# Attention units reordered and paced over half output steps, and a third pair's q through the crossbar

## The chip, the core and the metric

The kernel runs on one core of a Trainium2 chip. The metric is the device time of one launch in microseconds (us), taken as the median of several runs. TensorE (PE, with its weight loads shown as PEld), VectorE (DVE), ScalarE (ACT), GpSimd (POOL) and SyncE (SP, here a queue that issues DMAs) run side by side and wait for each other by semaphores.

## The reference

The inputs q, k and v have shape (4, 8, 768, 64): 4 batches, 8 heads, 768 rows, 64 columns. The rows form 8 blocks of 96. A small matrix `sort_net` (8 x 8 for each batch and head) becomes P by five rounds of row and column normalization. P mixes the blocks of k and of v, and each block of q attends to its mixed block. The result goes through a bilinear feed-forward network (FFN).

```python
k_sorted = einsum('bhij,bhjcd->bhicd', P, k_blocks)      # the same for v
attn = softmax(q_block @ k_sorted_block.T / sqrt(64))    # 96 x 96 in each block
x = (attn @ v_sorted_block)  ->  (4*768, 8*64)
out = ((x @ w_a) * (x @ w_b)) @ w_out                    # 512 -> 1536 -> 512
```

The matrix products run in bf16; sums are float32 in PSUM.

## The kernel before, in words

**The work.** Heads are taken in pairs. A pair has a number g = 4 * batch + pair, so batch 0 has g = 0 to 3 and batch 3 has g = 12 to 15. Batch 0 is computed in two halves of four blocks each (the `half_...` functions). Batches 1 to 3 take whole pairs, and each pair is cut into three units:

- `c_(g)`: `stage_mix` mixes k and v of the pair with P (12 + 12 matmuls into two PSUM tiles `mix`). ACT copies the k tile to `kT`; DVE and ACT copy one half each of the v tile to `vT`. For g > 4 SP then issues a DMA transpose (the crossbar) of `vT` into `vs`. For g = 4, 5 and 6 the unit begins with `turn_q`, which transposes q on PE by 12 matmuls into `q_ps` and copies it out on DVE. From g = 6 on POOL copies one element of `kT` into `gate`, which makes it wait, and then issues the loads of pair g + 2.
- `s_(g)`: `stage_scores` computes the scores in two halves of 8 matmuls, each into its own PSUM tile `sc`, and ACT takes the exponential of each. For g = 4 `turn_v` transposes v on PE.
- `o_(g)`: `stage_o` multiplies by v in two halves of 8 matmuls, each into its own PSUM tile `o_ps`. For each half DVE takes a reciprocal (`rec`) and multiplies (`xp`), which empties the tile. `to_xT` then issues a DMA transpose of `xp` into `xT` on SP.

For pairs whose q goes by the crossbar, `pair_q` reorders q on POOL (tile `qc`) and `stage_q` issues its DMA transpose on SP (tile `qTf`). Before, that holds for g = 7 to 15. `pair_q(7)` stands on POOL after the early loads, `stage_q(7)` in `s_(5)`, and for later pairs both stand in `o_(g-2)`.

**PSUM.** Pool `psA` has two slots of two banks. Every `mix`, `sc` and `o_ps` takes one, so each unit takes both, and a unit's first tile waits until the unit before has emptied its first tile, and likewise for the second. Pool `psF` has four slots of one bank for the FFN tiles `pf` and `po` and for `q_ps`.

**The FFN.** `ffn_ab(b, m, t)` is one step of 8 matmuls with 384 columns (4 for w_a, 4 for w_b); ACT copies the first product to `a_sb` and DVE multiplies it with the second into `hT`. `ffn_out(b, c)` is 12 matmuls with 512 columns into one `po`, which ACT (even c) or DVE (odd c) copies to `o_sb`, and SP stores it.

**Order.** PE, POOL and SP run in the written order. For the main part, `paced` goes through the steps of batch b's FFN and puts the 12 units of batch b + 1 among them. A step of `ab` counts 1 and a whole `ffn_out` counts 2. A unit is due when its share of the total is passed, and all units that are due after a step follow it at once. Before, the order of the units is c0 s0 c1 s1 o0 c2 s2 o1 c3 s3 o2 o3. ACT and DVE take their order in this part from a scheduler when the program is built.

**The begin of the FFN.** At the end of batch 0's first half five FFN accumulations are begun with three of their four matmuls: three in `psF` tiles and two in the halves of one `psA` tile named `two`. `ffn_ab` later adds the last matmul (line 332) to each.

Of the kernel before, what the change touches and what calls it, by code (L numbers as in the profile page):

```python
# [9 lines left out]
FP32 = mybir.dt.float32  # L10
# [6 lines left out]
def _ap(t: bass.AP, extra_offset, pattern):  # L17
    return bass.AP(tensor=t.tensor, offset=t.offset + extra_offset,
                   ap=[list(p) for p in pattern])
# [3 lines left out]
def kernel(  # L23
# [11 lines left out]
    nc = tc.nc  # L35
    P = 128
    B, H, S, D = q.shape
# [3 lines left out]
    DMODEL = H * D  # L41
# [4 lines left out]
    NCH = S // P  # L46
    HP = H // 2
    KA = DMODEL // P
    KO = DFF // P
# [17 lines left out]
    psA = ctx.enter_context(tc.tile_pool(name="psA", bufs=2, space=PSUM))  # L67
    psF = ctx.enter_context(tc.tile_pool(name="psF", bufs=4, space=PSUM))
# [19 lines left out]
    def load_pair(b, hp):  # L88
        tiles = []
        for name, t in (("k2", k), ("v2", v), ("q2", q)):  # L90
            base = (b * H + 2 * hp) * S * D
            if b == 0 and name == "q2":
                continue
            to = ld.tile([P, 2, W], BF16, tag=name, name=name)
            nc.gpsimd.dma_start(out=to, in_=_ap(t, base, [[W, P], [S * D, 2], [1, W]]))  # L95
            tiles.append(to)
        loaded[b * HP + hp] = tiles
# [3 lines left out]
    w_out_sb = const.tile([P, KO, DMODEL], BF16, name="w_out_sb")  # L101
# [8 lines left out]
    def load_out(c):  # L110
        nc.gpsimd.dma_start(
            out=w_out_sb[:, c * 4:(c + 1) * 4, :],
            in_=moe_w_out.rearrange("(kc p) n -> p kc n", p=P)[:, c * 4:(c + 1) * 4, :])
# [46 lines left out]
    def copy(eng, out, in_):  # L160
        if eng == "act":
            nc.scalar.copy(out=out, in_=in_)  # L162
        else:
            nc.vector.tensor_copy(out=out, in_=in_)  # L164
# [79 lines left out]
    def pair_q(g):  # L244
        qc = qtp.tile([P, NCH, 2, D], BF16, tag="qc", name="qc", bufs=4)
        nc.gpsimd.tensor_copy(out=qc.rearrange("p c e d -> p e c d"),  # L246
                              in_=loaded[g][2].rearrange("p e (c d) -> p e c d", c=NCH))
        st[g, "qc"] = qc

    def stage_q(g):  # L250
        qT = qtp.tile([P, NCH, P], BF16, tag="qTf", name="qTf", bufs=4)
        nc.sync.dma_start_transpose(out=qT, in_=st[g, "qc"].rearrange("p c e d -> p (c e d)"))
        st[g, "qT"] = qT

    def turn_q(g, eng="dve"):
        q2 = loaded[g][2] if g >= HP else q_first[:, 2 * g:2 * g + 2]
        q_ps = psF.tile([P, NCH, P], BF16, tag="F", name="q_ps")
        for c in range(NCH):
            for e in range(2):
                nc.tensor.matmul(q_ps[e * D:(e + 1) * D, c, :],  # L260
                                 lhsT=q2[:, e, c * D:(c + 1) * D],
                                 rhs=ident, is_transpose=True)
        qT = qtp.tile([P, NCH, P], BF16, tag="qT", name="qT")
        copy(eng, qT, q_ps)
        st[g, "qT"] = qT

    def turn_v(g):
        vT, vs = vTs[g % NBUF], vss[g % NBUF]
        vs_ps = psF.tile([P, NB, P], BF16, tag="F", name="vs_ps")
        for i in range(NB):  # L270
            nc.tensor.matmul(vs_ps[:, i], lhsT=vT[:, i], rhs=ident, is_transpose=True)
        nc.vector.tensor_copy(out=vs[0:BLK, :, V0:V0 + P], in_=vs_ps[0:BLK])
# [37 lines left out]
    def stage_o(g):  # L310
        xp = att.tile([BLK, NB, 2, D], BF16, tag="xp", name="xp")
        for hf in range(2):
            one_o(eTs[g % NBUF], hf, vss[g % NBUF], hf * NBH, xp, NB)
        st[g, "xp"] = xp
# [8 lines left out]
    hTs = {}  # L323
# [32 lines left out]
    def ffn_last(b, c):  # L356
        hT = hTs[b]
        rows = out[b * S:(b + 1) * S, :].rearrange("(p c) n -> c p n", c=NCH)
        for n0, n1, eng, queue in ((0, 384, "act", nc.sync), (384, DMODEL, "dve", nc.scalar)):
            po = psF.tile([P, 512], FP32, tag="F", name="po")  # L360
            for m in range(KO):
                nc.tensor.matmul(po[:, 0:n1 - n0], lhsT=hT[:, m, c * P:(c + 1) * P],  # L362
                                 rhs=w_out_sb[:, m, n0:n1], start=(m == 0), stop=(m == KO - 1))
            o_sb = ffp.tile([P, 512], FP32, tag="o_sb", name="o_sb", bufs=3)
            copy(eng, o_sb[:, 0:n1 - n0], po[:, 0:n1 - n0])
            queue.dma_start(out=rows[c][:, n0:n1], in_=o_sb[:, 0:n1 - n0])

    def ffn_out(b, c):
        if b == B - 1 and c == NCH - 1:
            ffn_last(b, c)  # L370
            return
        hT = hTs[b]
        po = psF.tile([P, DMODEL], FP32, tag="F", name="po")
        for m in range(KO):
            nc.tensor.matmul(po, lhsT=hT[:, m, c * P:(c + 1) * P], rhs=w_out_sb[:, m, :],  # L375
                             start=(m == 0), stop=(m == KO - 1))
        o_sb = ffp.tile([P, DMODEL], FP32, tag="o_sb", name="o_sb", bufs=3)
        copy("act" if c % 2 == 0 else "dve", o_sb, po)
        if b == 0:
            h, u = divmod(c, 3)  # L380
            for c2 in range(2):
                nc.sync.dma_start(
                    out=_ap(out, (h * PH * NCH + 2 * u + c2) * DMODEL,
                            [[NCH * DMODEL, PH], [1, DMODEL]]),
                    in_=o_sb[c2 * PH:(c2 + 1) * PH])
        else:
            rows = out[b * S:(b + 1) * S, :].rearrange("(p c) n -> c p n", c=NCH)
            nc.sync.dma_start(out=rows[c], in_=o_sb)


    with tc.manual_schedule(engines={ET.PE, ET.Pool, ET.SP}):
        with tc.manual_schedule(engines={ET.Activation, ET.DVE}):
# [7 lines left out]
            for it in range(5):  # L400
# [15 lines left out]
                if it > 0:  # L416
                    nc.tensor.matmul(heat[0:NB, 1, 0:NB], lhsT=rsum, rhs=rsum,
                                     start=True, stop=True)
# [59 lines left out]
            half_x(0, 2, "act")  # L478
            half_o(0, 3)
            begun = [psF.tile([P, 512], FP32, tag="F", name="pf") for _ in range(3)]  # L480
            two = psA.tile([P, 2, 512], FP32, tag="A", name="two")
            begun += [two[:, 0], two[:, 1]]
            for n, (m, w_sb) in enumerate(((0, w_a_sb), (0, w_b_sb), (1, w_a_sb),
                                           (1, w_b_sb), (2, w_a_sb))):
                if n == 3:
# [9 lines left out]
        load_pair(1, 3)  # L495
        for c in range(3):
            load_out(c)
        pair_q(2 * HP - 1)
        for g in range(2, 4):
            spread(nc.gpsimd, p_col, g * 8, 8)  # L500
# [22 lines left out]
        def units_full(b):  # L523
            g0, us = b * HP, []

            def c_(g):
                if g < 2 * HP - 1:
                    turn_q(g)
                stage_mix(g, "k", ("act",))
                stage_mix(g, "v", ("dve", "act"))  # L530
                if 2 * HP - 2 <= g < B * HP - 2:
                    nc.gpsimd.tensor_copy(out=gate, in_=kTs[g % NBUF][0:1, 0:1])  # L532
                    load_pair((g + 2) // HP, (g + 2) % HP)

            def s_(g):
                stage_scores(g)
                if g == HP:
                    turn_v(g)
                if g == HP + 1:
                    stage_q(2 * HP - 1)  # L540

            def o_(g):
                stage_o(g)
                to_xT(g)
                if 2 * HP <= g + 2 < B * HP:
                    pair_q(g + 2)
                    stage_q(g + 2)

            for n in range(HP + 1):
                if n < HP:  # L550
                    us.append(lambda g=g0 + n: c_(g))
                    us.append(lambda g=g0 + n: s_(g))
                if n > 0:
                    us.append(lambda g=g0 + n - 1: o_(g))
            return us

        def interleave(steps, units, spare, slow=0):
# [6 lines left out]
                    done += 1  # L564

        def paced(ab, po, units, spare):
            steps = [(1, f) for f in ab] + [(2, f) for f in po]
            total = sum(t for t, f in steps) - 2 * spare
            now = done = 0
            for t, step in steps:  # L570
                step()
                now += t
                while done < len(units) and done * total < now * len(units):
                    units[done]()
                    done += 1

        steps = [lambda: ffn_ab(0, 0, 0, begun[0:2]), lambda: ffn_ab(0, 1, 0, begun[2:4]),
                 lambda: ffn_ab(0, 2, 0, begun[4:5])]
# [3 lines left out]
        for b in range(B):  # L582
            ab = [lambda m=m, t=t, b=b: ffn_ab(b, m, t)
                  for m in range(KO) for t in range(2) if b > 0 or t == 1]
            po = [lambda c=c, b=b: ffn_out(b, c) for c in range(NCH)]
            paced(ab, po, units_full(b + 1) if b + 1 < B else [], 3 if b == 0 else 2)


# [28 lines left out]
```

## Time and profile before

| | |
|---|---|
| median of 3 runs | 247.38 us (247.31 to 247.84) |
| the profiled execution: its time, its span | 247.31 us, 245.5 us |
| PE busy | 236.9 us, 96% of the span |
| PEld, DVE, ACT, POOL busy | 137.5, 109.1, 104.4, 60.6 us |
| granted TensorE clock, mean | 1.000 |

The span runs from the first to the last instruction; 1.8 us of the execution's time lie outside it. A busy share is an average over the whole span. Which engine bounds a stage is read from the chain of waits, which follows the work that ended last back to its start, and from the waits of PE in that stage.

### The profile page before, as it was taken

To read this page: it belongs to the slowest core of one execution; us is meant where nothing else is said; L and a number is where in the kernel's file an instruction comes from. 1 tells how busy PE (TensorE), PEld (TensorE's weight loads), DVE (VectorE), ACT (ScalarE), POOL (GpSimd) and SP (SyncE) were. 2 spreads that over 40 slices of the span, in tenths; PEclk is the share of its full clock that TensorE was granted. 3 is DMA by queue.
4 is the path that set the end of the run, shared out by engine and by line. 5 is a ranking of instruction groups with operands and counts; after the bars stand their busy time and mean duration, and the time that the engine had idled before them with its cause. 6 is when DMAs were issued, how large, how long until landed. Compare 5 with 4: busy or idle time off the path is not lost.

```text
span 245.5 us, 5508 instructions
## 1 busy us (share of the span) xinstructions
PE 236.9 (96%) x2246; PEld 137.5 (56%) x2258; DVE 109.1 (44%) x259; ACT 104.4 (43%) x204; POOL 60.6 (25%) x87
## 2 busy tenths in 40 slices
PE   7888899999989999999999999999999999999995
PEld 2466566666645456666645466666645465665443
DVE  6674366656435243463616144454516144443210
ACT  3664764465651046545440055555540033333001
POOL 8876477700323021404041032210000000000000
PEclk9999999999999999999999999999999999999999
DMA  5999999946859968939394936934333310000122
GB/s 81 201 199 197 197 199 202 206 73 77 143 107 202 151 138 133 137 70 136 70 144 124 217 69 115 138 66 45 64 89 117 117 45 0 0 3 1 43 107 106
DMA packets 53129, 27.82 MB, mean 113 GB/s; under 512 B 29936, under 2 KB 50160, under 8 KB 53104
## 3 DMA queue, kind: packets, MB, share of 16 engines
q0 software_dynamic: 20944, 14.16, 40.7%
q1 hardware_dynamic: 32016, 13.25, 24.7%
q8 instruction: 17, 0.28, 0.4%
q10 hardware_dynamic: 144, 0.07, 0.1%
q14 instruction: 8, 0.07, 0.1%
HBM read 28.32 MB, written 6.29 MB: 141 GB/s over the span
## 4 chain that ended last, share of the span: by engine, by line
PE 94%; DVE 3%; issue 1%; ACT 1%
PE pf L332 51%; PE po L375 24%; PE mix L281 4%; PE o_ps L231 3%; PE heat L168 2%; PE sc L302 2%; PE mixh L180 2%; PE po L362 1%; PE vs_ps L208 1%; PE sc L195 1%; PE xt_ps L222 1%; PE q_ps L260 1%; PE two L332 1%; PE mixh L168 0%; ACT qT L162 0%
## 5 line engine op out<-in xcount | busy, mean ns | idle before, releaser
L353 DVE TENSOR_TENSOR hT<-a_sb,pf 128x384 bf16<-128x384 bf16 x95 | 52.6, 553 | 73.6 <-PE pf L332 48.5
L332 PE MATMUL pf<-xT,w_a_sb 128*128 128x384 bf16 x380 | 77.8, 326 | 0.0
L332 PE MATMUL pf<-xT,w_b_sb 128*128 128x384 bf16 x380 | 77.4, 326 | 0.0
L352 ACT CAST a_sb<-pf 128x384 bf16<-128x384 f32 x95 | 45.5, 479 | 62.1 <-PE pf L332 40.8
L375 PE MATMUL po<-w_out_sb,hT 128*128 128x512 bf16 x265 | 60.5, 379 | 0.7 <-issue 0.2
L332 PEld LDWEIGHTS <-w_b_sb 128*128 128x128 bf16 x384 | 37.5, 98 | 25.2 <-issue 0.6
L332 PEld LDWEIGHTS <-w_a_sb 128*128 128x128 bf16 x384 | 34.9, 98 | 22.2
L375 PEld LDWEIGHTS <-hT 128*128 128x128 bf16 x276 | 26.3, 97 | 30.3
L162 ACT COPY o_sb<-po 128x512 f32<-128x512 f32 (+1 forms) x13 | 7.5, 578 | 50.0 <-PE po L375 48.6
L164 DVE COPY o_sb<-po 128x512 f32<-128x512 f32 (+1 forms) x12 | 7.9, 658 | 44.3 <-PE po L375 38.7
L307 ACT ACTIVATE eT<-sc 96x768 bf16<-96x768 f32 x24 | 18.1, 803 | 3.2 <-PE sc L302 3.2
L532 POOL COPY gate<-kT 1x1 bf16<-1x1 bf16 x8 | 1.4, 179 | 68.8 <-ACT kT L162 68.8
L237 DVE TENSOR_TENSOR xp<-o_ps,rec 96x512 bf16<-96x512 f32 x24 | 15.7, 683 | 0.2
L162 ACT CAST kT<-mix 128x384 bf16<-128x384 f32 x24 | 10.3, 482 | 8.1 <-PE mix L281 8.1
L95 POOL DMA_DIRECT2D k<-in_k_dram x16 | 11.6, 726 | 5.1 <-PE pf L332 2.3
L95 POOL DMA_DIRECT2D v<-in_v_dram x16 | 11.5, 721 | 2.5 <-PE pf L332 0.7
L231 PEld LDWEIGHTS <-eT 96*128 96x128 bf16 x256 | 10.4, 97 | 2.7 <-issue 0.2
L246 POOL COPY qc<-q 128x768 bf16<-128x768 bf16 x9 | 7.6, 840 | 17.3 <-DMA q<-in_q_dram 17.3
L231 PE MATMUL o_ps<-vs,eT 96*128 96x65 bf16 x256 | 11.2, 193 | 0.0
L95 POOL DMA_DIRECT2D q<-in_q_dram x12 | 8.7, 721 | 1.6 <-DMA w_a_sb<-in_moe_w_a_dram 0.7
L168 PE MATMUL heat<-warm 128*128 128x512 bf16 x20 | 7.6, 527 | 1.4 <-DVE warm L77 1.3
L164 DVE CAST vT<-mix 128x384 bf16<-128x384 f32 x12 | 6.7, 558 | 3.9 <-PE mix L281 3.8
(80 smaller groups left out, 154.0 us busy)
## 6 DMA issues: line engine op xcount, KB each, us to landing
out_dram<-o_sb SPq DMA_DIRECT2D x17, 256.0 KB, 2.0
k<-in_k_dram POOLq DMA_DIRECT2D x16, 192.0 KB, 5.1
v<-in_v_dram POOLq DMA_DIRECT2D x16, 192.0 KB, 6.3
q<-in_q_dram POOLq DMA_DIRECT2D x12, 192.0 KB, 6.4
w_a_sb<-in_moe_w_a_dram POOLq DMA_DIRECT2D x6, 256.0 KB, 10.1
w_b_sb<-in_moe_w_b_dram POOLq DMA_DIRECT2D x6, 256.0 KB, 10.4
w_out_sb<-in_moe_w_out_dram POOLq DMA_DIRECT2D x3, 512.0 KB, 10.0
out_dram<-o_sb SPq DMA_DIRECT2D x12, 128.0 KB, 2.4
```

What stands on the lines that cost most here:

```text
L95: nc.gpsimd.dma_start(out=to, in_=_ap(t, base, [[W, P], [S * D, 2], [1, W]]))
L162: nc.scalar.copy(out=out, in_=in_)
L164: nc.vector.tensor_copy(out=out, in_=in_)
L168: nc.tensor.matmul(ps[:, 0:cols], lhsT=warm[:, 0:P], rhs=warm[:, 0:cols], start=True, stop=True)
L231: nc.tensor.matmul(o_ps[:, e, i * (D + 1):(i + 1) * (D + 1)], lhsT=eT[:, hf, e, i * BLK:i * BLK + P], rhs=vs[0:BLK, i0 + i, V0 - 1 + e * ( ...
L237: nc.vector.tensor_tensor(out=_ap(xp, i0 * 2 * D, [[nxp * 2 * D, BLK], [D, 2], [2 * D, NBH], [1, D]]), in0=_ap(o_ps, 1, [[1024, BLK], [511 ...
L281: nc.tensor.matmul(mix[e * D:(e + 1) * D, c // 3, c % 3 * P:(c % 3 + 1) * P], lhsT=src2[:, e, c * D:(c + 1) * D], rhs=s_all[:, 2 * g + e], ...
L307: nc.scalar.activation(out=eT[:, hf, :, 0:HB], in_=sc[0:BLK, :, 0:HB], func=AF.Exp, scale=float(scale))
L332: nc.tensor.matmul(pf[:, 0:HW], lhsT=w_sb[:, kc, m * P:(m + 1) * P], rhs=x_cols(b, kc, t), start=(kc == 0), stop=(kc == KA - 1))
L352: nc.scalar.copy(out=a_sb, in_=pf[:, 0:HW])
L353: nc.vector.tensor_mul(out=hT[:, m, t * HW:(t + 1) * HW], in0=a_sb, in1=ab[1][:, 0:HW])
L375: nc.tensor.matmul(po, lhsT=hT[:, m, c * P:(c + 1) * P], rhs=w_out_sb[:, m, :], start=(m == 0), stop=(m == KO - 1))
```

## The change

1. `ffn_out` becomes two steps of 6 matmuls each on the same `po`, and the store follows the second. `paced` counts every step 1, so a unit can fall between two halves.
2. The order of the units becomes c0 s0 c1 s1 c2 o0 s2 c3 o1 s3 o2 o3: the third and the fourth mix each come one unit sooner.
3. q of g = 6 no longer goes through `turn_q`: `pair_q(6)` comes before `pair_q(7)` on POOL and `stage_q(6)` into `s_(4)`.
4. For g >= 8 `pair_q` and `stage_q` move from `o_(g-2)` to `s_(g-1)`.
5. The two begun accumulations that shared one `psA` tile `two` take a tile each, both named `two`.

```diff
     def ffn_out(b, c):
         if b == B - 1 and c == NCH - 1:
-            ffn_last(b, c)
-            return
-        hT = hTs[b]
-        po = psF.tile([P, DMODEL], FP32, tag="F", name="po")
-        for m in range(KO):
-            nc.tensor.matmul(po, lhsT=hT[:, m, c * P:(c + 1) * P], rhs=w_out_sb[:, m, :],
-                             start=(m == 0), stop=(m == KO - 1))
+            return [lambda: ffn_last(b, c)]
+        held = {}
+
+        def part(n):
+            if n == 0:
+                held["po"] = psF.tile([P, DMODEL], FP32, tag="F", name="po")
+            for m in range(n * KO // 2, (n + 1) * KO // 2):
+                nc.tensor.matmul(held["po"], lhsT=hTs[b][:, m, c * P:(c + 1) * P],
+                                 rhs=w_out_sb[:, m, :], start=(m == 0), stop=(m == KO - 1))
+            if n == 1:
+                store(b, c, held["po"])
+
+        return [lambda: part(0), lambda: part(1)]
+
+    def store(b, c, po):
         o_sb = ffp.tile([P, DMODEL], FP32, tag="o_sb", name="o_sb", bufs=3)
...
-            two = psA.tile([P, 2, 512], FP32, tag="A", name="two")
-            begun += [two[:, 0], two[:, 1]]
+            begun += [psA.tile([P, 2, 512], FP32, tag="A", name="two")[:, 0] for _ in range(2)]
...
+        pair_q(2 * HP - 2)
         pair_q(2 * HP - 1)
...
             def c_(g):
-                if g < 2 * HP - 1:
+                if g < 2 * HP - 2:
                     turn_q(g)
...
                 if g == HP:
                     turn_v(g)
-                if g == HP + 1:
-                    stage_q(2 * HP - 1)
+                if g in (HP, HP + 1):
+                    stage_q(g + 2)
+                if 2 * HP <= g + 1 < B * HP:
+                    pair_q(g + 1)
+                    stage_q(g + 1)
 
             def o_(g):
                 stage_o(g)
                 to_xT(g)
-                if 2 * HP <= g + 2 < B * HP:
-                    pair_q(g + 2)
-                    stage_q(g + 2)
-
-            for n in range(HP + 1):
-                if n < HP:
-                    us.append(lambda g=g0 + n: c_(g))
-                    us.append(lambda g=g0 + n: s_(g))
-                if n > 0:
-                    us.append(lambda g=g0 + n - 1: o_(g))
+
+            for u, n in ((c_, 0), (s_, 0), (c_, 1), (s_, 1), (c_, 2), (o_, 0), (s_, 2), (c_, 3),
+                         (o_, 1), (s_, 3), (o_, 2), (o_, 3)):
+                us.append(lambda u=u, g=g0 + n: u(g))
             return us
...
         def paced(ab, po, units, spare):
-            steps = [(1, f) for f in ab] + [(2, f) for f in po]
-            total = sum(t for t, f in steps) - 2 * spare
-            now = done = 0
-            for t, step in steps:
+            steps = ab + po
+            total = len(steps) - 2 * spare
+            done = 0
+            for now, step in enumerate(steps, 1):
                 step()
-                now += t
                 while done < len(units) and done * total < now * len(units):
...
-            po = [lambda c=c, b=b: ffn_out(b, c) for c in range(NCH)]
+            po = [f for c in range(NCH) for f in ffn_out(b, c)]
```

## The prediction

> **What bounds the kernel now.** I read the page's head and its chain of waits first, to learn which engine sets the end; then PE's own waits in the main part, to learn where that engine stands still; then the chain piece by piece around those places.
>
> ```profile
> span 245.5 us, 5508 instructions
> PE 236.9 (96%) x2246; PEld 137.5 (56%) x2258; DVE 109.1 (44%) x259; ACT 104.4 (43%) x204; POOL 60.6 (25%) x87
> ...
> PE 94%; DVE 3%; issue 1%; ACT 1%
> ```
>
> PE is busy for 96% of the span and holds 94% of the chain. The rest of the chain is mostly the first 12 us, which the change does not touch. So time can only come from PE work taken away or from PE waits taken away. PE's waits from 28 us to the end:
>
> ```profile
> PE sc L302 <- ACT kT L162: 0.7, 1, 0.7
> PE sc L302 <- ACT vT L162: 0.2, 1, 0.2
> PE po L375 <- issue: 0.2, 1, 0.2
> ```
>
> All three belong to one place, 70 to 73 us. In the table of windows PE is busy 54.34 of 54.50 us in batch 1's FFN (86.8 to 141.3) and 54.44 of 54.60 in batch 2's: nothing is to be had there. Before 28 us one wait matters here, 0.6 us of `two` (line 332) for DVE's `hT`. The chain in order of time (start, duration, what):
>
> ```profile
> 26.29 0.52 PE mixh L180 x24
> 26.81 0.55 DVE hT L353
> 27.35 0.04 issue
> 27.39 0.32 PE two L332
> 27.72 0.65 PE pf L332 x4
> ...
> 60.37 0.46 PE q_ps L260 x12
> 60.83 0.67 PE mix L281 x24
> ...
> 70.44 0.81 PE mix L281 x24
> 71.25 0.02 issue
> 71.28 0.57 DVE vT L164
> 71.84 0.02 issue
> 71.87 0.49 ACT vT L162
> 72.36 0.04 issue
> 72.40 0.35 PE sc L302 x8
> 72.75 0.16 issue
> 72.90 2.54 PE po L375 x11
> ...
> 88.09 0.79 PE mix L281 x24
> ```
>
> At 26.8 PE stands until DVE has read the other half of the same tile. At 60.4 the transposes of q take 0.46 us of PE. At 70.4 c7 is followed at once by s7: a whole `ffn_out` counts 2, so two units came due together, and s7 finds both `psA` slots still being emptied. At 88.1 stands the price of a mix that needs no transposes.
>
> **The change part by part.**
>
> *q of g = 6 by the crossbar.* The q_ps and mix pieces of c6 took 0.46 + 0.67 = 1.13 us; a mix alone takes 0.79. PE gains **0.34 us**. The 0.55 us copy of `q_ps` leaves DVE, off the path. What is added: a copy on POOL (0.84 us by line 246) and a transpose on SP (1.24 us of SP, landing 2.8 to 4.4 us after issue). On POOL it stands where `qc` of g = 7 already waited 3.37 us for its load, until 44.71; if that cover were gone, 0.84 us would move the last two `s_all` spreads (45.50 to 49.46), first used at 88. Cost nothing. On SP it precedes the first `vs` transpose, issued at 55.16; with q copied by about 46 it has landed by 51, and s6 comes near 64. Cost nothing.
>
> The Trainium skill, "TensorE: Matmul & The Clock Gate", Part 4 (PE-mode transpose), gives about 275 ns for a 128x128 bf16 transpose inside a kernel, and by that the 12 would be an estimated 3.3 us and the change worth some 3 us more. The trace shows 12 of them (64-column weights, 128 columns out) in 0.46 us of chain, 38 ns each, since they overlap; the single row's 223 ns is latency, and I go by the chain.
>
> *Units over half steps, and the mix one unit sooner.* For batch 0 there are 12 + 12 steps, total 24 - 6 = 18, so the units fall after steps 1, 2, 4, 5, 7, 8, 10, 11, 13, 14, 16, 17, with one or two steps (1.30 us each: 8 matmuls of `pf`, or half of the 2.59 us of a `po`) between neighbours. Before, units 9 and 10 fell together. They took 70.44 to 72.75 = 2.31 us; c7 and s7 apart cost 0.79 + 0.45 = 1.24 (pieces at 88.09 and 64.20). That frees 1.07; but c7 is now followed by FFN steps, and a step after a mix takes 1.41 instead of 1.30 (pieces at 64.65 and 66.55; the one after scores shows the same). PE gains **0.96 us**.
>
> *`two` as two tiles.* The last matmul into the second half then need not wait for DVE's reading of the first. From the end of the mixes (26.81) to the next `pf` (27.72) is 0.91 us; one matmul after a mix takes 0.27 (the piece at 25.86). PE gains **0.64 us**. Next late could be the scores at 28.37, moved to 27.73: they need the slot of the first `two`, free when DVE ends at 27.36, so they do not wait. The second tile's slot is that of the last first-half `o_ps`; its reader `xph` also feeds the transposes at 23.44, which PE passes first, so no wait is added.
>
> Sum of the gains: 0.34 + 0.96 + 0.64 = 1.94 us.
>
> *New waits.* In batch 1 four pairs of neighbours now stand one step apart that did not: c6-o4, s6-c7, o5-s7, o6-o7. Each needs both `psA` slots of its predecessor.
> - c6-o4: after c7's start (70.44) ACT ended its part of `vT` at 72.35, 1.9 us later; o4's second half starts 0.79 + 1.41 + 0.25 = 2.45 after c6. No wait.
> - s6-c7: exponentials of s6 ended at 66.02, 1.82 after its start at 64.20; c7's second mix starts 0.45 + 1.41 + 0.4 = 2.26 after. No wait.
> - o5-s7: o7's last multiplication ended at 79.89 + 0.69 = 80.58, 2.05 after its start (78.53). s7's second half would start at 0.50 + 1.30 + 0.23 = 2.03, and a release takes 0.05 more (72.35 to 72.40): a wait of 0.07.
> - o6-o7: store 1's copy on DVE (0.69 us) still stands ahead of o6's reciprocals. In the trace o6 had just that: start 75.44, last multiplication ended at 77.59, 2.15 later. o7's second half would start at 0.50 + 1.30 + 0.25 = 2.05: a wait of 0.15.
>
> A wait also costs the restart: the 8 scores after one took 0.35 instead of 0.23, and 0.16 of issue followed. I take 0.1 for each, so **0.4 us** in all. From below it is 0 (both waits are of the size of my rounding); below nothing I exclude, since no PE work leaves by it. From above, DVE can have one more FFN multiplication (0.55) ahead in each: 0.4 + 1.1 = 1.5. I take 0.4, as the rows above are the same instructions in the same order.
>
> *q one unit sooner for g >= 8.* On POOL `qc` waits for its load, and behind it stand the `gate` and the loads of the next pair. For g = 8 the order is gate of c7, its three loads, `qc`, as it was (74.23, no wait); the q load of pair 8 is issued some 2 us earlier than before, c6 being earlier, and lands in 5 to 6.5 us. For g = 10 to 12 `qc` came after the next pair's loads without a wait (99.85, 112.21, 124.56) and has the same place. The 4.2 and 4.86 us that POOL waited at 79.26 and 130.28 become work of the next batch's first unit, hidden behind its loads. On SP `qTf` for g = 9 is issued some 5 us after c8's start (kT 1.1, gate and three load issues 2.7, copy 0.86) and lands 3 us later; s9 starts eight steps and three units, some 12 us, after c8. Nothing waits. If one did, `vs` and `xT` transposes and stores stand behind it on SP.
>
> *Batches 2 and 3.* 36 steps, total 32: units after steps 1, 3, 6, 9, 11, 14, 17, 19, 22, 25, 27, 30, never closer than two steps (2.6 us), against 2.15 us for the slowest emptying. The counts of mixes, scores and outputs among the steps are the same. Cost nothing. `xT`'s last transpose is issued near 78 in batch 1, before it was 82.39, and the FFN step that first reads it comes near 85.3, before it was 86.80: more room.
>
> Net: 1.94 - 0.4 = 1.5 us. The profiled execution took 247.31 (span 245.5 and 1.81 around it), so 245.8; the median of the runs is 0.07 above it, within the rounding: **245.8 us**.
>
> **The rivals.**
>
> *No new wait at all.* For it: the two waits rest on differences of 0.02 and 0.10 us. Then all of 1.94 stays: 245.4. Chance 0.17.
>
> *Half of it is given back.* The order of DVE puts FFN multiplications ahead in o5 and o6, or `two`'s wait is followed by another in the half stage, whose tiles also turn over in `psF`. Waits of 1.0 to 1.45: 246.4 to 246.9. Chance 0.10.
>
> *Only the transposes' share stays*, because the stall at 71 us moves to the new neighbours and the one at 27 us to the next tile: 247.38 - 0.34 = 247.0, no measurable change. Chance 0.08.
>
> *Slower: the two `psA` slots become the bound in batch 1.* Place: the four one-step pairs, 58 to 77 us. Price: at distance zero one pair cost 1.07 us, so 4.3 at most, against 1.94 gained: 249.7. It decides against the change when each pair waits over 0.61 us, that is when each emptying ends 0.6 us later than its second tile is wanted. For it: DVE serves FFN multiplications (0.55), vT, and outputs in one line, and PE follows at once. Against: two of the four have 0.45 us of room by the rows above. Chance 0.07.
>
> **How the numbers follow.** Forecast 0.58, no new wait 0.17, half given back 0.10, unchanged 0.08, slower 0.07. A change of 0.2%, 0.5 us, is about what a measurement of this kernel can tell from none. Faster than 246.9 are the first three: 0.85; within: 0.08; slower: 0.07. The range goes from 245.2 (no new wait, 0.11 saved at `two` where a restarted matmul is read as an ordinary one, and 0.11 after c7 not paid) to 246.9 (new waits at their upper bound of 1.5).
>
> **What would show it.** In the profile after: no `q_ps` pieces between 55 and 65 us; the mix near 65 followed by `pf`, not by scores; no PE wait for ACT's `kT`; no wait of `two` for `hT`; PE waits for DVE `xp` of 0.05 to 0.3 at s7 and o7, near 71 and 76; the first `pf` of the next batch's FFN near 85.3 instead of 86.80; and the chain from there as long as before. It is wrong if PE waits for a `qTf` or `vs` transpose, or if PE's waits after 28 us add up to more than 1 us.

## The result and the profile after

| | before | changed |
|---|---|---|
| median of 6 runs | 247.19 us (246.59 to 247.84) | 245.80 us (245.78 to 246.84) |
| the profiled execution: time, span | 247.31 us, 245.5 us | 246.84 us, 245.1 us |

The ratio of changed to before is 0.9951, 95% interval 0.9929 to 0.9974: faster by 0.3 to 0.7%, or 0.6 to 1.8 us. The forecast was 245.8 us, a gain of 1.5.

The head of the page and PE's own waits from 28 us on, after:

```profile
span 245.1 us, 5487 instructions
PE 236.8 (97%) x2234; PEld 137.1 (56%) x2246; DVE 109.4 (45%) x258; ACT 104.5 (43%) x204; POOL 61.4 (25%) x88
```

```profile
PE o_ps L231 <- DVE xp L237: 0.2, 1, 0.2
```

PE is still the bound. The three waits at 70 to 73 us are gone from this list; one new wait of 0.2 us stands in it, and it is o7's for the slot that o6's `xp` empties. The chain in order of time shows the rest (start, duration, what):

```profile
27.30 0.27 PE two L332
27.57 0.65 PE pf L332 x4
...
46.60 0.46 PE q_ps L260 x12
...
58.42 0.79 PE mix L281 x24
...
65.56 0.79 PE mix L281 x24
66.35 1.41 PE pf L332 x8
...
70.84 0.29 PE sc L302 x8
71.14 0.02 issue
71.16 0.34 PE sc L302 x8
...
74.23 0.69 DVE o_sb L164
...
75.11 1.26 DVE xp L237 x2
...
76.41 0.42 PE o_ps L231 x8
...
85.89 1.30 PE pf L332 x8
```

`two` (27.30) starts where the mixes end, with no DVE piece between, c6 (58.42) and c7 (65.56) cost 0.79 each, and c7 is followed by an FFN step. At s7 the two halves of the scores are split by a short wait. At o7 the chain leaves PE for DVE: the copy of store 1, the reciprocals and the multiplications of o6 stand in a line, and o7's second half starts when they end.

Since every run shifts the first 25 us a little, I compare stretches of the chain that start and end at the same work in both kernels. The rows of before that bound the batch 1 stretch, with o7 between them:

```profile
46.76 0.46 PE q_ps L260 x12
...
75.94 2.59 PE po L375 x12
78.53 0.50 PE o_ps L231 x16
...
86.80 1.30 PE pf L332 x8
```

| stretch | before | after | difference |
|---|---|---|---|
| end of the mixes to the next `pf`, near 27 us | 26.81 to 27.72 = 0.91 | 27.30 to 27.57 = 0.27 | -0.64 |
| c4's start to the first FFN step of the next batch (batch 1) | 46.76 to 86.80 = 40.04 | 46.60 to 85.89 = 39.29 | -0.75 |
| the same FFN's start to the next one's (batch 2) | 86.80 to 141.32 = 54.52 | 85.89 to 140.42 = 54.53 | 0 |
| and once more (batch 3) | 141.32 to 195.85 = 54.53 | 140.42 to 194.94 = 54.52 | 0 |

In the profiled executions PE gained 0.64 + 0.75 = 1.39 us in these stretches. The two profiled executions differ by only 0.47 us because the one of the changed kernel lost 0.5 us ahead of 25 us and 0.5 us after its last copy, in code that the change does not touch; the other five runs of the changed kernel took 245.78 to 245.82 us.

### The profile page after: what moved, and what is told of

It is laid out like the page before. It is cut to its first block, busy times and chain, and to the rows that moved or that the text cites. A ratio compares the mean times of both kernels' runs of the same rounds, so it can differ in the third digit from the quotient of the medians.

```text
span 245.1 us, 5487 instructions
## 1 busy us (share of the span) xinstructions
PE 236.8 (97%) x2234; PEld 137.1 (56%) x2246; DVE 109.4 (45%) x258; ACT 104.5 (43%) x204; POOL 61.4 (25%) x88
## 4 chain that ended last, share of the span: by engine, by line
PE 92%; DVE 4%; issue 1%; ACT 1%; DMA 1%
PE pf L332 51%; PE po L377 24%; PE mix L281 4%; PE o_ps L231 3%; PE sc L302 2%; PE mixh L180 2%; PE po L362 1%; PE vs_ps L208 1%; PE sc L195 1%; PE xt_ps L222 1%; DMA p_nat<-in_sort_net_dram 1%; PE heat L168 1%; PE two L332 1%; PE q_ps L260 1%; DVE xp L237 1%
## 5 line engine op out<-in xcount | busy, mean ns | idle before, releaser
L377 PE MATMUL po<-w_out_sb,hT 128*128 128x512 bf16 x265 | 61.3, 379 | 0.6
L95 POOL DMA_DIRECT2D v<-in_v_dram x16 | 11.5, 722 | 3.5 <-DMA w_b_sb<-in_moe_w_b_dram 1.8
L235 DVE RECIPROCAL rec<-o_ps 96x8 f32<-96x8 f32 x32 | 5.6, 189 | 13.8 <-PE o_ps L231 13.8
L246 POOL COPY qc<-q 128x768 bf16<-128x768 bf16 x10 | 8.4, 843 | 7.5 <-DMA q<-in_q_dram 7.5
```

Source lines behind the costliest of these rows:

```text
L377: nc.tensor.matmul(held["po"], lhsT=hTs[b][:, m, c * P:(c + 1) * P], rhs=w_out_sb[:, m, :], start=(m == 0), stop=(m == KO - 1))
```

## The experiments

The prediction summed three parts of the change as if each were worth its own PE time. The rival reading is that they depend on each other. All ratios below are to the kernel before, on the same chip, with their 95% intervals; "the batch 1 stretch" is the second row of the table.

### Each part alone

**`two_only`**: the kernel before with only this edit:

```diff
-            two = psA.tile([P, 2, 512], FP32, tag="A", name="two")
-            begun += [two[:, 0], two[:, 1]]
+            begun += [psA.tile([P, 2, 512], FP32, tag="A", name="two")[:, 0] for _ in range(2)]
```

> The kernel before, with only the two begun accumulations in a psA tile each. Three-gains theory (each part of the change takes its own PE time): 0.64 us faster than before; in the chain the last matmul into the second two takes 0.27 us after the mixes near 27 us, with no wait for hT; the pieces at 60 and 70 us stay as before (q_ps 0.46 + mix 0.67; c7 and s7 2.31). Moved-stall theory: the wait goes to the scores or the vs transposes behind it, PE's waits before 30 us stay at 0.6, time as before.

Measured: 246.52 us, ratio 0.9959 (0.9942 to 0.9975): a gain of 0.6 to 1.4 us. After the mixes `two` takes 0.27 us, as expected, and no wait follows it. But in the profiled execution the batch 1 stretch is longer than the 40.04 us of before: it runs from 45.56 to 85.93 and takes 40.37, 0.33 us more. PE's waits and the chain name the place:

```profile
PE o_ps L231 <- DMA vs<-vT: 0.2, 1, 0.2
```

```profile
71.19 6.18 DMA vs<-vT
...
77.51 0.65 PE o_ps L231 x16
```

o7 now waits for the transpose of g = 7's v, issued at 71.19 and in the chain for 6.18 us. In the kernel before, SP issued it here:

```profile
72.40 1.29 SPq L292 DMA_TRANSPOSE vs<-vT  x1
```

It landed 5.8 us later, at 78.2, and PE came to o7 at 78.53, 6.1 us after the issue: 0.3 us of room were left, and no wait showed. `two` stands ahead of the issue, so it moves the issue and o7 alike, and the 6.1 us between them are the same in both kernels. What differs is the landing, 6.2 us instead of 5.8. That the edit brings this about is not shown. The gain of the runs has room for the forecast 0.64 and none for 0.64 - 0.33 = 0.31.

**`q_only`**: the kernel before with only q of g = 6 by the crossbar:

```diff
+        pair_q(2 * HP - 2)
         pair_q(2 * HP - 1)
...
-                if g < 2 * HP - 1:
+                if g < 2 * HP - 2:
                     turn_q(g)
...
-                if g == HP + 1:
-                    stage_q(2 * HP - 1)
+                if g in (HP, HP + 1):
+                    stage_q(g + 2)
```

> The kernel before, with only q of g = 6 by POOL and the crossbar. Three-gains theory: 0.34 us faster; c6 takes 0.79 in place of 1.13, the wait at 70 us and the one of two stay. Late-q theory: s6 near 64 waits for qTf, or POOL's added copy holds back a later step; time as before or above. If the 12 transposes cost what a lone one costs (0.22 us by their rows), 2.6 us faster.

Measured: 247.32 us, ratio 1.0003 (0.9991 to 1.0016): nothing gained. The batch 1 stretch is 46.24 to 86.36 = 40.12. Neither theory foresaw why. The chain:

```profile
59.85 0.97 PE mix L281 x24
...
77.86 0.08 issue
77.94 0.65 PE o_ps L231 x16
```

c6 takes 0.97 instead of 0.79: in the old order o4 stands one step ahead of it, and without the 0.46 us of transposes between them its second tile comes before o4's slot is free. The rest goes at o7, where 0.50 becomes 0.08 + 0.65. The profile lists no wait there, but the `vs` transpose, issued at 71.72, took 6.1 us to land, and PE came to o7 just as long after the issue: again a landing 0.3 us longer than before, where before had 0.3 us of room. In the changed kernel c6 costs 0.79: there scores, two steps back, stand ahead of it and not outputs one step back.

**`halves_only`**: the old order of units, only `ffn_out` in two steps and every step counted 1 (part 1 of the change, as in its diff).

> The kernel before in the old order of units, with only the output steps halved and counted 1 each. Three-gains theory: c7 and s7 come apart, 0.96 us less there; o6 and o7 now stand one step apart with store 1's copy on DVE between, which costs 0.32 as in the changed kernel; net 0.6 us faster, and o5 and s7 are not neighbours, so no wait at s7. Order theory (the new order is what takes the stall away): under 0.2 us faster, since a wait for the psA slots stays near 70 us.

Measured: 247.13 us, ratio 0.9984 (0.9969 to 0.9999). c7 and s7 do come apart (c7 costs 0.79 at 68.87), but the batch 1 stretch is 46.48 to 86.34 = 39.86, a gain of 0.18 where some 0.6 was expected:

```profile
70.80 5.69 DMA vs<-vT
...
76.62 0.65 PE o_ps L231 x16
```

The wait for `vs` at o7 is 0.6 us by PE's waits, larger than the one for `xp` that I had expected. Here the cause is in the edit: the stall that it takes away stood between the issue of the transpose and o7. PE now comes to o7 5.2 us after the issue instead of 6.1, and the landing took 5.7.

The same two times in six profiles (room: from the issue of `vs` of g = 7 until PE has done the work ahead of o7; landing: from the issue to the arrival):

| kernel | issue | room | landing | wait for `vs` |
|---|---|---|---|---|
| before | 72.40 | 6.1 | 5.8 | none |
| `two_only` | 71.19 | 6.1 | 6.2 | 0.2 |
| `q_only` | 71.72 | 6.1 | 6.1 | 0.1 by the chain |
| `halves_only` | 70.80 | 5.2 | 5.7 | 0.6 |
| `old_order` (below) | 70.48 | 5.2 | 5.9 | 0.8 |
| changed | 67.49 | 8.5 | 7.0 | none |

The three parts alone change the batch 1 stretch and `two` together by -0.31, +0.08 and -0.18 us. Their sum is -0.41; the change as a whole gives -1.39. But the profile of `two_only` stands apart: these stretches give it 0.31 and the medians of the runs 0.81, while for every other kernel here except `q_late` the two agree within 0.2 us (`halves_only` 0.18 and 0.20). With `two` at its 0.64 the sum is -0.74. What the runs show to depend on other parts is the rest: q and the half steps, priced at 0.34 and 0.96 ahead of the new waits, give 0.10 alone.

### The order of the units

**`old_order`**: the changed kernel with only the order undone:

```diff
-            for u, n in ((c_, 0), (s_, 0), (c_, 1), (s_, 1), (c_, 2), (o_, 0), (s_, 2), (c_, 3),
-                         (o_, 1), (s_, 3), (o_, 2), (o_, 3)):
+            for u, n in ((c_, 0), (s_, 0), (c_, 1), (s_, 1), (o_, 0), (c_, 2), (s_, 2), (o_, 1),
+                         (c_, 3), (s_, 3), (o_, 2), (o_, 3)):
```

> The changed kernel with the units in the order of the kernel before (c0 s0 c1 s1 o0 c2 s2 o1 c3 s3 o2 o3), all other parts kept. Transpose theory (the earlier parts are worth something only because the new order issues the vs transpose of g = 7 sooner): from c4's start c7 begins at 22.2 us and vs is issued 1.9 later; it lands 5.7 after that, o7 cannot start before 30.0, so the FFN after it starts 39.7 us after c4's start against 39.3 in the changed kernel; PE waits some 1 us at o7 for vs. 0.4 us slower than the changed kernel, 1.0 faster than before. Independent-parts theory (the prediction, which priced the order at nothing but its new waits): o7 waits 0.3 for xp, s7 not at all; 0.2 faster than the changed kernel.

Measured: 246.61 us, ratio 0.9982 (0.9972 to 0.9993). The batch 1 stretch is 46.33 to 86.24 = 39.91, 0.62 more than in the changed kernel (0.4 expected):

```profile
PE o_ps L231 <- DMA vs<-vT: 0.8, 1, 0.8
```

```profile
59.93 0.97 PE mix L281 x24
...
68.56 0.79 PE mix L281 x24
...
70.48 5.90 DMA vs<-vT
...
76.52 0.65 PE o_ps L231 x16
```

With every other part in place and only the old order, o7 waits 0.8 us for `vs`, and c6 takes 0.97 instead of 0.79, as in `q_only`. In the new order c7 starts 19.0 us after c4 (65.56 - 46.60) instead of 22.2 (68.56 - 46.33), the transpose is issued at 67.49, and o7 is due at 76.01, 8.5 us later; no wait for `vs` is left, though the landing took 7.0. This supports the transpose theory. No run here keeps the old order and takes the transpose off the path, so the price of this wait by itself is read and not tested; nor was a shorter landing tried.

**`whole_steps`**: the changed kernel, but with whole output steps counted 2 as before.

```diff
-            po = [f for c in range(NCH) for f in ffn_out(b, c)]
+            def whole(c, b=b):
+                for f in ffn_out(b, c):
+                    f()
+            po = [lambda c=c, w=whole: w(c) for c in range(NCH)]
```

with `paced` as in the kernel before.

> The changed kernel with the output steps whole again and counted 2, the rest of the change kept. Three-gains theory: o5 and s7 fall due together after the first output step; s7's second half waits until o5's last multiplication, 2.05 us after o5's start instead of 0.5: 1.65 lost there, 0.2 and 0.3 of waits at s7 and o7 no longer paid, so 1.1 us slower than the changed kernel, 0.3 faster than before. Order theory: no slower than the changed kernel, 1.4 faster than before.

Measured: 247.00 us, ratio 0.9982 (0.9969 to 0.9994). The batch 1 stretch is 45.56 to 85.81 = 40.25, 0.96 more than in the changed kernel. o5 and s7 now fall due together, and the wait has moved from ACT's `vT` to DVE's `xp`:

```profile
PE sc L302 <- DVE xp L237: 1.3, 2, 0.8
```

So the order does not take the stall away by itself; the half steps do.

**`q_late`**: the changed kernel with part 4 undone (`pair_q` and `stage_q` of g >= 8 back behind `to_xT` in `o_(g-2)`).

> The changed kernel with pair_q and stage_q of g >= 8 back in o_(g-2) behind to_xT. Load-bearing theory: in the new order s2 and s3 then follow o0 and o1 by three steps, while the q transpose is issued behind that of xT some 3.4 us after the o unit starts and lands 3 to 4 later; s10, s11, s14 and s15 each wait 2 to 3 us for qTf, 8 to 12 us slower than the changed kernel. No-matter theory (the prediction's reading that q has room anywhere): as the changed kernel.

Measured: 258.33 us, ratio 1.0469 (1.0441 to 1.0498).

```profile
PE sc L302 <- DMA qTf<-qc: 9.2, 4, 2.4
```

```profile
108.21 1.01 DVE xp L237 x2
...
109.93 0.77 SPq L318
...
110.79 3.32 DMA qTf<-qc
```

Four scores wait up to 2.4 us each. In this trace SP issues in the written order: the transpose of q stands behind that of `xp`, which must first be computed, and only then come 3.3 us until it lands. With s2 three steps after o0 that is too late. The gain and this loss belong to the same change: without part 4 it would have been 4.7% slower than the kernel before.

The waits are not the whole loss. The mean granted clock was 0.993 in the profiled execution and 0.980 to 0.987 in the other five; in the profile it was 0.89 between 130 and 145 us, where the changed kernel had 1.00. By these means I estimate the slower clock at 0.7% to 2% of some 256 us, 1.8 to 5 us in a run. Whether the waits bring it about was not tested.

### The new waits

**`act_store`**: the changed kernel with store 1 of batch 0's FFN copied by ACT.

```diff
-        copy("act" if c % 2 == 0 else "dve", o_sb, po)
+        copy("act" if c % 2 == 0 or (b, c) == (0, 1) else "dve", o_sb, po)
```

> The changed kernel with the copy of store 1 of batch 0's FFN on ACT instead of DVE. DVE-line theory: o6's reciprocals no longer stand behind the 0.69 us copy, its last multiplication ends 2.05 us after its start, and the wait of o7 falls from 0.32 us (with restart) to under 0.1; s7's 0.2 stays; 0.3 us faster than the changed kernel. If the wait at o7 is one for a transpose or for issue, nothing changes.

Measured: 245.70 us, ratio 0.9955 (0.9932 to 0.9977). The batch 1 stretch is 45.57 to 84.75 = 39.18, a gain of 0.11, not 0.3. DVE's own line of instructions shows why:

```profile
73.45 0.20 DVE L235 RECIPROCAL rec<-o_ps 96x8 f32<-96x8 f32 x1 [3.38 <-PE o_ps L231]
...
74.52 0.69 DVE L237 TENSOR_TENSOR xp<-o_ps,rec 96x512 bf16<-96x512 f32 x1
```

o6 started at 73.17 and its last multiplication ended at 74.52 + 0.69 = 75.21, 2.04 us later even without the copy in front; o7's second half wants the slot 2.05 us after. No wait is listed any more, but that half still starts only at the release and its 8 matmuls take 0.42 us (75.27) instead of 0.25: the restart is paid all the same. With the copy in front the multiplication ended 2.15 us after o6's start (74.21 to 76.36). Of the 0.69 us copy 0.28 had lain in time in which DVE would have waited for PE, and behind the copy the reciprocals and multiplications stand close together and take 1.44 us instead of 1.77 (73.45 to 75.22).

**`spare2`**: the changed kernel with the units of batch 1 spread over 20 half steps instead of 18.

```diff
-            paced(ab, po, units_full(b + 1) if b + 1 < B else [], 3 if b == 0 else 2)
+            paced(ab, po, units_full(b + 1) if b + 1 < B else [], 2)
```

> The changed kernel with two spare outputs instead of three in batch 0's pacing: units after steps 1, 2, 4, 6, 7, 9, 11, 12, 14, 16, 17, 19, so that o5-s7 and o6-o7 stand two steps apart. Slot theory: both waits (0.21 at s7, 0.32 at o7) go, 0.5 us faster than the changed kernel, near 245.3. Late-output theory: o7 comes two steps later, its xT transpose ends some 5 us after it, and the next batch's FFN waits for it or its store queue; no gain or slower.

Measured: 245.48 us (245.22 to 245.74), ratio 0.9934 (0.9922 to 0.9947). The batch 1 stretch is 46.08 to 84.82 = 38.74, 0.55 less than in the changed kernel, and the chain stays on PE:

```profile
72.91 0.45 PE sc L302 x16
...
74.76 0.49 PE o_ps L231 x16
...
77.84 0.49 PE o_ps L231 x16
```

Both waits are gone at once, which confirms that 0.5 us lay in the two together. This version has the lowest median of the study; the two intervals, both against the kernel before, still overlap, so that it beats the changed kernel is shown by the stretch and not by the times.

## Why the prediction was right

**The sum.** Forecast: gains of 1.94, new waits of 0.4, net 1.5. Measured in the chain: 1.39; by the runs 0.6 to 1.8. The main forecast, that PE is relieved at three places and pays a little at two, is what happened. That the 245.8 was met to the digit is luck: the kernel before had a median of 247.19 here, not 247.38, and the gain was 0.1 smaller. Why the three gains could all be had at once is a matter of luck too, as told below.

**q of g = 6: 0.34.** c6 fell from 1.13 to 0.79, as priced; in the old order it falls only to 0.97. The 275 ns for a transpose in a kernel of the Trainium skill, "TensorE: Matmul & The Clock Gate", Part 4 (PE-mode transpose), would by the prediction's estimate have made this some 3 us more; the trace's chain price held. The cover on POOL and SP held too, with less room than was said: `qTf` for g = 6 was issued at 42.77 and took 10.5 us to land, so it was there at 53.3 and not by 51, and s6 at 63.7 did not wait.

**Half steps: 0.96.** The batch 1 stretch gained 0.75, so with 0.34 for q and 0.53 of new waits, 0.94 are left for the half steps. Undoing them costs 0.96 (`whole_steps`; 1.1 was expected there), but that equal figure is another sum: a larger stall at o5 and s7 comes in, and the new waits go out. (The piece at 64.65 that the prediction gives for a step after a mix follows scores; after c7 it took 1.41 as well, at 66.35.)

**`two`: 0.64.** Measured 0.64 at its place, alone and with the rest.

**New waits: 0.4.** They came where they were put, and cost somewhat more. At s7 the scores took 0.29 + 0.02 + 0.34 and a gap, 70.84 to 71.50 = 0.66 instead of 0.45: 0.21. At o7 the first matmul was due at 74.21 + 0.50 + 1.30 = 76.01 and the last ended at 76.83, not 76.51: 0.32. Together 0.53; `spare2` won back 0.55. The waits proper are as forecast, 0.09 at s7 (71.16 against 71.07) and 0.15 at o7 (76.41 against 76.26); the restart, taken as 0.1 each, was sized too small: the 8 matmuls behind each wait took 0.34 and 0.42 us where 0.22 and 0.25 were due.

**The step that was missing.** The mix one unit sooner was given no price of its own, and the prediction nowhere weighed the `vs` transpose of g = 7 as the next thing to come late; it names a wait for `vs` only as a sign of being wrong. In the kernel before that transpose had 0.3 us of room at o7. The half steps take 0.9 us out of the time between its issue and o7, so in the old order most of their gain turns into a wait for it. In all, 0.62 us of the gain (39.91 against 39.29) hangs on the order: it saves 0.18 at c6 and the wait at o7 with its restart, 0.84 + 0.15, and it brings the new waits of 0.53. The forecast sum came out because the new order issues the transpose sooner in the same change, which the prediction had not reckoned with. Taken one by one, the prices of q and of the half steps would have been wrong.

**Where "Nothing waits" was right but said too little.** The move of `pair_q` and `stage_q` was read as harmless and also as without use. `q_late` shows that the new order needs it: 4.7% slower without.

**The rivals.** No new wait at all: refuted by 0.53 us of waits. Half given back, or only the transposes' share: not so; the new waits came to 0.53 us and not to 1.0 or more, and neither stall moved, since distance and order changed together (`whole_steps` and `old_order` each bring one back). Slower by the `psA` slots: two of the four pairs did wait, for 0.2 and 0.3 us, far from 0.61 each; o4 after c6 (0.49) and c7 after s6 (0.79) took their usual time without a wait, as the rows of before had said.

## What to carry to other kernels

A wait that does not show in the profile can still be next in line: before pricing a gain on the bounding engine, look for transfers that land close to the moment they are wanted (here 0.3 us ahead of it). Time won between such a transfer's issue and its use is lost there unless it is issued sooner too; time won ahead of the issue moves both. When units share two PSUM slots, the price of a neighbour is how long its emptying takes, here about 2.1 us against the distance between their matmuls, and one step more between two such pairs was worth 0.55 us. Parts that look separate can each be worth little alone, as q and the half steps were here, and their full price together, so a part should be judged with the others in place. And one profiled execution may not stand for the others, as that of `two_only` seems not to: compare its stretches with the medians of the runs.

## What the runs showed of the hardware

A float32 copy on DVE near 11.5 us (`p_rep`, 256 elements in 32 partitions) took 0.28 to 0.30 us in six of the ten profiles and 0.51 to 0.57 in the other four. In those four it started 0.27 to 0.31 us after POOL had begun to issue a DMA (11.71 against 11.44 in the changed kernel); in the kernel before it started 0.12 after (11.59 against 11.47) and took 0.28, and the other starts, 0.08 before to 0.02 after the issue's begin or 0.53 and more after it, gave 0.28 to 0.30 too. All four long copies ended 0.08 to 0.10 us after the issue did. The Trainium skill, "SBUF — State Buffer", "SBUF: two separate sides", says that a DVE operation in a perf mode with two ports and a GpSimd operation lock each other out of a shared pair of ports, whoever starts first, for the whole instruction; it names a float32 copy within SBUF as one that uses this mode. The longer copies fit such a lock only in part: the copy that started 0.12 us into an issue of 0.74 us was not held up. No run here separates the lock from other causes. The longer copy moves the work behind it by up to 0.3 us from profile to profile, as much as some of the edits.

PE's stop for "issue" near 18 us, in code that no kernel here changed, took between 0.50 us (`two_only`) and 1.04 us (the changed kernel). Together these make the differences of single profiled times, such as the 0.47 us between the two main ones, too coarse to read an edit of 0.3 us from; the stretches between the same pieces of work agree to 0.01 us where the kernels do not differ (batches 2 and 3 in the table).
